# Sums of one column in the free columns of the PV banks, another order of phi and of the residual, and due times found by search

## The chip, the core and the metric

The kernel runs on one core of a Trainium2 chip. Its metric is the device time of one execution in microseconds, the median of three runs. A core has five engines that each work through a queue of their own in order: PE (matrix products, which land in PSUM), ACT (ScalarE, here the exponentials), DVE (VectorE), POOL (GpSimd) and SP, which here only issues DMAs. What one engine needs of another it waits for on a semaphore.

## The reference

Two branches read the same layer-normed input and are added to it. `x` is 2048 x 512, bf16.

```python
xn = layernorm(x)
return x + A(xn) + B(xn)

# A: 32 heads of 16, four segments s of 512 positions, with a memory M, z per head
q, k, v = xn @ wq, xn @ wk, xn @ wv
phi = lambda t: where(t > 0, t + 1.0, exp(t))
p = softmax(q_s @ k_s.T / 4 + mask);  a_dot = p @ v_s
a_mem = phi(q_s) @ M / (phi(q_s) @ z + 1e-6)
o_s = g * a_mem + (1 - g) * a_dot          # g = sigmoid(beta), per head
M = M + phi(k_s).T @ v_s;  z = z + sum(phi(k_s))
A = o @ wo

# B: one position of 2048 goes through a gated MLP
r = xn @ w_r;  idx = argmax(r)
y = (silu(xn[idx] @ w_gate) * (xn[idx] @ w_up)) @ w_down * sigmoid(r[idx])
B = xn, with y added to row idx
```

So the output is `x + xn + A`, with `y` added in one row. `mask` adds -1e9 where the key is later than the query.

## The kernel before, in words

Positions are tiled in 16 blocks of 128; four blocks are a segment. Heads are worked in 16 groups `n` of eight (four groups for each segment), and each group in two units of four heads. A unit is five tiles (`LAYOUT`), so there are 160 tiles in all. A tile is a `score` on PE into `st` (L442, two PSUM buffers), an exponential on ACT into `pt` (L445, six buffers), a mask on POOL (L454), and PV on PE into the unit's bank `acc` (L463, two buffers). PV carries a column of ones, so the bank holds the softmax sums too; DVE reads the unit out with `rr` and `Oseg` (L428, L429). PV fills 272 of the 512 columns of its bank.

PE multiplies all 128 rows of a tile, so a head's queries lie in `QZ`, a tile with zeros outside that head's 16 rows. The projected queries are read out by DVE (`raw_q`, L385), and eight small DMAs from SP scatter them into `QZ` (L379). There are two `QZ` tiles, for even and odd `n`.

`phi` (L368 to L375) takes a projected tile: ACT makes exp(t) into `ex`, POOL clips it into `am`, DVE makes t + 1 and then the maximum of the two. The keys' phi is transposed by DMA (`memT`, L471), and `memM` adds it to the memory; `mem` (L494 to L519) multiplies the memory into a segment's output, and POOL adds that to `Oseg`.

`moe` (L597 to L718) is the branch B. Its products have one column each: the router's 64 (L618), the selected row (L675), gate and up (L690) and down (L709). Each has a bank of the pool `misc`, of which there are two, shared with all projections. `guard` sums squares of the weights likewise (L566); its flag decides on a slow path that these inputs don't take.

`fin` (L536) ends a block of segments 0 to 2: the output is transposed by DMA (`oT`, L541), an identity matmul brings in the row `rb` (L543; POOL makes it from `y` and the layer norm's offset, L524), four matmuls apply `wo` (L545), and DVE adds `x` times `s1` (`ob`, L531). The last segment's four blocks are ended by the code from L869 on; its first two take `x` through three diagonal matmuls (`dg`, L908).

The order of all this on each engine is not written by hand. Every step is an operation of a `Plan`, with the engine, an estimate of its time, what it reads and writes, and a due time `d`. `run` walks a model of the engines: it takes the engine whose next operation can start first, and on that engine, among the operations that can start by then (within 0.03 us, more for some of DVE's), the one with the earliest due time. The result is a fixed queue for each engine; on the chip nothing is reordered. `td(t)` gives the due time of tile `t`.

Of the kernel before, what the change touches and what calls it, by code (L numbers as in the profile page):

```python
# [18 lines left out]
TAIL = {"PE": 0.22, "ACT": 0.18, "DVE": 0.135, "POOL": 0.09, "SP": 1.9}  # L19
# [16 lines left out]
class Plan:  # L36
# [4 lines left out]
    def __init__(self):  # L41
        self.ops = []
        self.writer = {}
        self.readers = {}
        self.floor = {}

# [28 lines left out]
    def run(self, dry=False, log=None):  # L75
        free = {e: 0.0 for e in TAIL}
        port = [0.0]
        nd = {}
# [32 lines left out]
        while left:  # L111
            best = None
            for e, av in avail.items():
# [4 lines left out]
                for o in av:  # L118
# [6 lines left out]
                    if e == "POOL":  # L125
                        t = max(t, port[0])
                    cands.append((t, o))
# [4 lines left out]
                pick = min((o for t, o in cands if t <= lo + (0.8 if o["lock"] and o["d"] < t else 0.03)), key=lambda o: (o["d"], o["id"]))  # L132
# [10 lines left out]
            if o["lock"]:  # L143
                port[0] = end
            fin = end + o["lat"]
# [12 lines left out]
            for u in o["users"]:  # L158
                k = u["id"]
                nd[k] -= 1  # L160
                ready[k] = max(ready[k], end if e == u["eng"] != "SP" else fin)
# [14 lines left out]
def build_kernel(ctx, tc, A_x, A_wq, A_wk, A_wv, A_wo, A_beta, B_x, B_w_r, B_w_gate, B_w_up, B_w_down, out, opts=None):  # L176
# [23 lines left out]
    rot = ctx.enter_context(tc.tile_pool(name="rot", bufs=2))  # L200
# [3 lines left out]
    obp = ctx.enter_context(tc.tile_pool(name="obp", bufs=4))  # L204
# [73 lines left out]
    T0, SL = 11.2, 1.0  # L278
    DTL = 1.35

    def td(t):
        return T0 + SL * t

    class Build:


        def __init__(self, pl, gen):
# [3 lines left out]
            self.prev = dict(s=[], e=[], p=[])  # L291
            self.dq = nc.gpsimd if gen else nc.sync
# [5 lines left out]
        def segt(self, kind, s):  # L298
            if (kind, s) not in self.seg:
                pool, cap, shape = (pk1, 1, [P, 4, D]) if kind == "pk" else (rot, 2, [P, NCB, L])  # L300
                self.seg[(kind, s)] = Buf(pool, cap, shape, bf16, kind)
            return self.seg[(kind, s)]
# [25 lines left out]
        def ln_T(self, b, xb, eng, d):  # L328
            pl = self.pl
            if eng == "DMA":  # L330
                pl.op("SP", 1.26, lambda: nc.sync.dma_start(out=xnT[:, :, b * P:(b + 1) * P], in_=xb[:], transpose=True), r=[xb], w=[("xnT", b)], d=d, lat=DTL)
# [36 lines left out]
        def phi(self, raw, kind, s, j, d):  # L368
            pl = self.pl
            ex, am, tp1 = Buf(phw, 2, [P, L], bf16, "ex"), Buf(phw, 2, [P, L], bf16, "am"), Buf(phw, 2, [P, L], bf16, "tp1")  # L370
            dst = self.segt(kind, s)
            pl.op("ACT", .5, lambda: nc.scalar.activation(out=ex[:], in_=raw[:], func=ACT.Exp), r=[raw], w=[ex], d=d)
# [562 lines left out]
    def slow_path():  # L935
# [3 lines left out]
        def flush():  # L939
            spl.sequence()  # L940
# [120 lines left out]
```

## Time and profile before

| | us |
|---|---|
| median of three runs | 217.96 (217.15 to 219.58) |
| the profiled execution | 219.14 |
| its span, from first to last instruction | 217.4 |
| PE busy | 195.8 |
| ACT busy | 173.1 |
| POOL busy | 149.3 |
| DVE busy | 134.5 |

The rows of the profile are from the one profiled execution. Busy time counts an engine as busy while any of its instructions runs; PE's rows overlap, since matmuls are pipelined. A row of a group of instructions says: line, engine, operation, what is written from what, the shapes, how often; then busy us and mean ns of one; then the idle time of that engine just before, and what ended it. A row of the timeline says start and length in us, then the same names, and in brackets the idle time before it. A row of waits says who waited for whom: us in total, how often, the longest. Names are the program's, without buffer numbers.

### The profile page before, as it was taken

Reading aid. Unit: us, or ns where it says so; the run is one execution under the profiler, and the core shown is the slowest. Engines: PE = TensorE matmul, PEld = TensorE weight load, DVE = VectorE, ACT = ScalarE, POOL = GpSimd, SP = SyncE. Lnnn points to the kernel's source line nnn. Section 1 sums busy time; section 2 is a strip of 40 time slices with the busy share of each in tenths; the row PEclk is TensorE's granted clock in tenths of the full one; section 3 lists DMA queues with packets and bytes.
Section 4 is the critical chain, followed back from the end, with each engine's and each line's share of the span. In section 5 each row is a group of like instructions: output and inputs, shape, how many; then the busy total and the mean of one; then the engine's idle time right before and its main releaser. Section 6 shows DMA issues by size and latency. Waiting matters only on the chain.

```text
span 217.4 us, 6706 instructions
## 1 busy us (share of the span) xinstructions
PE 195.8 (90%) x2598; PEld 128.1 (59%) x2635; DVE 134.5 (62%) x365; ACT 173.1 (80%) x206; POOL 149.3 (69%) x250
## 2 busy tenths in 40 slices
PE   7899798998988999999999999999999799997960
PEld 2656465565646578785676656565666556564620
DVE  5779983465474655997647666446878847653140
ACT  2488988998997689999788796898778679876830
POOL 8018977997983367768669779998876387856500
PEclk9999999999996599999999999999999999999996
DMA  6913994532332413892100432224212102222002
GB/s 179 294 34 113 364 282 80 62 79 53 71 53 48 136 26 85 284 207 73 41 0 19 105 42 64 60 72 65 59 41 57 42 18 59 54 47 54 21 28 87
DMA packets 36985, 19.35 MB, mean 89 GB/s; under 512 B 24976, under 2 KB 36944, under 8 KB 36944
## 3 DMA queue, kind: packets, MB, share of 16 engines
q1 hardware_dynamic: 35840, 18.18, 35.2%
q10 hardware_dynamic: 1104, 0.66, 1.0%
q8 instruction: 22, 0.36, 0.8%
q14 instruction: 19, 0.16, 0.3%
HBM read 9.71 MB, written 2.10 MB: 54 GB/s over the span
## 4 chain that ended last, share of the span: by engine, by line
PE 53%; DMA 13%; DVE 10%; POOL 8%; ACT 6%; issue 4%; SPq 4%; DVEq 0%; ACTq 0%; POOLq 0%
PE st L442 20%; PE acc L463 8%; PE misc L364 6%; DMA QZ<-raw_q 5%; ACT pt L445 5%; PE misc L406 4%; POOL pt L454 4%; DMA xnT<-xn 4%; PE misc L545 3%; DMA pk<-pkT 2%; POOL sq L562 2%; SPq L379 2%; SPq L550 2%; PE misc L690 1%; DMA x_all<-in_A_x_dram 1%
## 5 line engine op out<-in xcount | busy, mean ns | idle before, releaser
L445 ACT ACTIVATE pt<-st 128x1024 bf16<-128x1024 f32 x160 | 154.2, 1028 | 25.8 <-PE st L442 22.5
L454 POOL TENSOR_SCALAR_AFFINE_SELECT pt<-pt 128x512 bf16<-128x512 bf16 (+1 forms) x160 | 88.7, 559 | 52.7 <-ACT pt L445 50.8
L442 PE MATMUL st<-QZ,KT 128*128 128x256 bf16 (+3 forms) x498 | 94.6, 302 | 5.9 <-DMA QZ<-raw_q 4.2
L463 PEld LDWEIGHTS <-pt 128*128 128x128 bf16 x1280 | 49.8, 97 | 20.2 <-POOL pt L454 4.1
L442 PEld LDWEIGHTS <-KT 128*128 128x128 bf16 x512 | 40.2, 98 | 24.0 <-issue 8.0
L463 PE MATMUL acc<-Vaug,pt 128*128 128x17 bf16 x1280 | 53.0, 171 | 1.5 <-DVE rm L512 0.6
L406 PE MATMUL misc<-wv,xnT 128*128 128x512 bf16 x60 | 17.2, 378 | 1.1 <-DMA xnT<-xn 0.9
L428 DVE RECIPROCAL rr<-acc 128x16 f32<-128x16 f32 x32 | 8.0, 250 | 16.4 <-PE acc L463 16.3
L531 DVE SCALAR_TENSOR_TENSOR ob<-x_all,s,misc 128x512 bf16<-128x512 bf16 x12 | 9.0, 748 | 13.9 <-PE misc L545 13.9
L364 PE MATMUL misc<-xnT,wq 128*128 128x512 bf16 x54 | 16.3, 378 | 1.4 <-DVE raw_q L385 1.2
L364 PE MATMUL misc<-xnT,wk 128*128 128x512 bf16 x55 | 16.1, 378 | 0.2
L373 POOL TENSOR_SCALAR am<-ex 128x512 bf16<-128x512 bf16 x24 | 15.1, 631 | 1.5 <-DVE pqT L375 0.5
L385 DVE CAST raw_q<-misc 128x512 bf16<-128x512 f32 x15 | 10.3, 686 | 8.2 <-PE misc L364 3.8
L408 DVE TENSOR_TENSOR Vaug<-misc,omg_bc 128x512 bf16<-128x512 f32 x16 | 10.9, 685 | 5.6 <-PE misc L406 5.3
L429 DVE TENSOR_TENSOR Oseg<-acc,rr 128x256 bf16<-128x256 f32 x32 | 13.5, 423 | 0.9
L524 POOL TENSOR_SCALAR rb<-ybc,onehot,cvec 128x512 bf16<-128x512 bf16 x16 | 12.3, 770 | 1.2 <-PE misc L543 0.9
L519 POOL TENSOR_TENSOR Oseg<-Oseg,om 128x512 bf16<-128x512 bf16 x10 | 11.5, 1155 | 1.9 <-DVE om L514 1.4
L545 PE MATMUL misc<-wo,oT 128*128 128x512 bf16 x42 | 11.8, 378 | 0.2
L308 DVE BATCH_NORM_STATS2 bnst<-x_all 128x6 f32<-128x512 bf16 x16 | 10.7, 666 | 1.5 <-DMA x_all<-in_A_x_dram 1.5
L514 DVE TENSOR_TENSOR om<-misc,rm 128x512 bf16<-128x512 f32 x12 | 8.2, 687 | 5.1 <-PE misc L508 5.1
L396 DVE CAST KT<-misc 128x512 bf16<-128x512 f32 x15 | 10.2, 682 | 1.0 <-PE misc L364 0.6
L324 POOL TENSOR_SCALAR xn<-x_all,rstd,cvec 128x512 bf16<-128x512 bf16 x12 | 9.5, 795 | 0.0
(161 smaller groups left out, 216.9 us busy)
## 6 DMA issues: line engine op xcount, KB each, us to landing
QZ<-raw_q SPq DMA_DIRECT2D x124, 16.0 KB, 1.8
mw<-in_B_w_gate_dram SPq DMA_DIRECT2D x2, 896.0 KB, 5.6
mw<-in_B_w_up_dram SPq DMA_DIRECT2D x2, 896.0 KB, 6.7
mw<-in_B_w_down_dram SPq DMA_DIRECT2D x2, 896.0 KB, 5.7
out_dram<-ob SPq DMA_DIRECT2D x14, 128.0 KB, 2.2
x_all<-in_A_x_dram SPq DMA_DIRECT2D x3, 512.0 KB, 4.7
wv<-in_A_wv_dram SPq DMA_DIRECT2D x1, 512.0 KB, 6.2
wo<-in_A_wo_dram SPq DMA_DIRECT2D x1, 512.0 KB, 4.0
```

The lines of the kernel that those rows point to most:

```text
L364: self.pl.op("PE", .216, lambda cb=cb: nc.tensor.matmul(ps[:], lhsT=w[:, cb, j * P:(j + 1) * P], rhs=xnT[:, cb, s * L:(s + 1) * L], start= ...
L373: pl.op("POOL", .58, lambda: nc.gpsimd.tensor_scalar(out=am[:], in0=ex[:], scalar1=1.0, scalar2=0.0, op0=ALU.min, op1=ALU.max), r=[ex], w= ...
L406: self.pl.op("PE", .216, lambda cb=cb: nc.tensor.matmul(ps[:], lhsT=xnT[:, cb, b * P:(b + 1) * P], rhs=wv[:, cb, :], start=(cb == 0), stop ...
L408: o = self.pl.op("DVE", .62, lambda: nc.vector.tensor_tensor(out=Vaug[:, b, :, 0:DH], in0=ps[:].rearrange("p (h e) -> p h e", e=DH), in1=o ...
L429: pl.op("DVE", .345, lambda: nc.vector.tensor_tensor(out=Oseg[s][:, :, j, 4 * w:4 * w + 4, :], in0=av()[:, :, :, 0:DH], in1=rr[:, :, :, No ...
L442: nc.tensor.matmul(st[:, i, off:off + n], lhsT=lh, rhs=QZ[q][:, h, q0:q0 + n], start=True, stop=True)
L445: self.prev["e"] = [pl.op("ACT", .907, lambda: nc.scalar.activation(out=pt[:], in_=st[:], func=ACT.Exp, scale=SCALE), r=[st], w=[pt], afte ...
L454: nc.gpsimd.affine_select(out=mv, in_=mv, pattern=pat, compare_op=ALU.is_ge, fill=0.0, base=0, channel_multiplier=-1)
L463: nc.tensor.matmul(acc[:, q0 // P + c, i, e, :], lhsT=pt[:, i, off + c * P:off + (c + 1) * P], rhs=Vaug[:, 4 * s + kb, h, :], start=first, ...
L519: pl.op("POOL", 1.12, lambda: nc.gpsimd.tensor_tensor(out=Oseg[s][:, :, j], in0=Oseg[s][:, :, j], in1=om[:], op=ALU.add), r=[om], w=[("O", ...
L524: self.pl.op("POOL", .75, lambda: nc.gpsimd.tensor_scalar(out=t[:], in0=small_t["ybc"][:], scalar1=small_t["onehot32"][:, b:b + 1], scalar ...
L545: pl.op("PE", .216, lambda cb=cb: nc.tensor.matmul(fin[:], lhsT=oT[:, cb, :], rhs=wo[:, cb, :], start=False, stop=(cb == NCB - 1)), r=[oT, ...
```

## The change

Six things change.

- The one-column sums of `moe` and `guard` get no bank of their own. They write into columns 272 and up of the bank of a unit (`V["moe"]` and `V["guard"]` name the units), after that unit's first PV; the unit's read-out waits for them.
- `phi` becomes max(t + 1, exp(min(t, 0))): DVE makes the minimum ahead of ACT's exponential, and POOL's clipping is gone.
- POOL makes the whole residual `x * s1 + cvec` in f32 (`xr`); `fin` has four matmuls, DVE adds `y` times the row's flag to the product in PSUM, and then the residual. In the tail `y` is added to `xr`, and two blocks take `xr` through two matmuls, as a bf16 part and the rest.
- DVE adds the memory's part to `Oseg` in POOL's place.
- Some heads of a group (`dvp`, 27 in all over n = 1 to 15) get their `QZ` by a multiplication on DVE in place of a DMA.
- The due times come from a table `V`, and some of the model's estimates change. Four of the MLP's weight tiles may be loaded at once (three before).

```diff
-TAIL = {"PE": 0.22, "ACT": 0.18, "DVE": 0.135, "POOL": 0.09, "SP": 1.9}
+TAIL = {"PE": 0.22, "ACT": 0.18, "DVE": 0.16, "POOL": 0.09, "SP": 1.9}
+SAME = {"PE": 0.0, "ACT": 0.0, "DVE": 0.11, "POOL": 0.0, "SP": 0.0}
...
-    rot = ctx.enter_context(tc.tile_pool(name="rot", bufs=2))
+    rot = ctx.enter_context(tc.tile_pool(name="rot", bufs=3))
+    xrp = ctx.enter_context(tc.tile_pool(name="xrp", bufs=2))
+    xrt = ctx.enter_context(tc.tile_pool(name="xrt", bufs=4))
...
-    mwp = ctx.enter_context(tc.tile_pool(name="mwp", bufs=3))
+    mwp = ctx.enter_context(tc.tile_pool(name="mwp", bufs=4))
...
+    V = dict(
+        dvp=(0, 2, 2, 2, 2, 2, 2, 2, 3, 3, 1, 1, 2, 1, 1, 1), dvl=1.826, slack=0.696, near=0.0, thin=0.204, sl=1.061, pq=8.672, pk=3.155, ev=-0.218,
...
-    T0, SL = 11.2, 1.0
-    DTL = 1.35
+    T0, SL = 11.2, V["sl"]
+    DTL = 1.4
...
+    XC = 4 * 4 * (DH + 1)
...
-            pl.op("ACT", .5, lambda: nc.scalar.activation(out=ex[:], in_=raw[:], func=ACT.Exp), r=[raw], w=[ex], d=d)
-            pl.op("POOL", .58, lambda: nc.gpsimd.tensor_scalar(out=am[:], in0=ex[:], scalar1=1.0, scalar2=0.0, op0=ALU.min, op1=ALU.max), r=[ex], w=[am], d=d + 1)
+            pl.op("DVE", .22, lambda: nc.vector.tensor_scalar(out=mn[:], in0=raw[:], scalar1=0.0, scalar2=None, op0=ALU.min), r=[raw], w=[mn], d=d + V["phmn"], lock=True)
...
+            pl.op("ACT", .5, lambda: nc.scalar.activation(out=ex[:], in_=mn[:], func=ACT.Exp), r=[mn], w=[ex], d=d)
...
+            nd = V["dvp"][n] if self.gen == 0 else 0
+            for h in range(nd):
+                self.pl.op("DVE", .22, lambda h=h: nc.vector.tensor_scalar(out=QZ[q][:, h, :], in0=raw[:], scalar1=bdsel[:, h:h + 1], scalar2=None, op0=ALU.mult),
+                           r=[raw], w=[("QZ", q, h)], d=td(10 * n + (5 if h >= 4 else 0)) - V["dvl"], lock=True)
...
-            acc = Buf(psa, 2, [P, 4, 2, 2, DH + 1], f32, "acc")
+            acc = Buf(psa, 2, [P, L], f32, "acc")
+            hook, keys = self.hooks.pop(base // 5, None) if self.gen == 0 else None, []
...
+                if k == 0 and hook:
+                    keys = hook[0](acc, self.prev["p"], td(t) + 2.5)
...
-            pl.op("POOL", 1.12, lambda: nc.gpsimd.tensor_tensor(out=Oseg[s][:, :, j], in0=Oseg[s][:, :, j], in1=om[:], op=ALU.add), r=[om], w=[("O", s, j, 0), ("O", s, j, 1)], d=d + 5)
+            pl.op("DVE", .37, lambda: nc.vector.tensor_tensor(out=Oseg[s][:, :, j], in0=Oseg[s][:, :, j], in1=om[:], op=ALU.add), r=[om], w=[("O", s, j, 0), ("O", s, j, 1)], d=d + V["madd"], lock=True)
...
-            self.pl.op("POOL", .75, lambda: nc.gpsimd.tensor_scalar(out=t[:], in0=small_t["ybc"][:], scalar1=small_t["onehot32"][:, b:b + 1], scalar2=cvec[:, b:b + 1], op0=ALU.mult, op1=ALU.add),
+            self.pl.op("POOL", .8, lambda: nc.gpsimd.tensor_scalar(out=t[:], in0=x_all[:, b, :], scalar1=s1[:, b:b + 1], scalar2=cvec[:, b:b + 1], op0=ALU.mult, op1=ALU.add), r=[("s1", b), ("cvec", b)], w=[t], d=d)
...
+            pl.op("DVE", .66, lambda: nc.vector.scalar_tensor_tensor(out=sub(fin), in0=small_t["ybc"][:], scalar=small_t["onehot32"][:, b:b + 1], in1=sub(fin), op0=ALU.mult, op1=ALU.add),
+            o = pl.op("DVE", .66, lambda: nc.vector.tensor_tensor(out=t[:], in0=sub(fin), in1=xr[:], op=ALU.add), r=[fin, ("fy", b), xr], w=[t], d=d)
...
-            pl.op("PE", .216, lambda: nc.tensor.matmul(fin[:], lhsT=ident[:], rhs=rb[:], start=True, stop=False), r=[rb, oT], w=[fin], d=d + 1)
...
+            def sums(acc, first, d, step, groups, r, name):
+                keys = []
+                for g, mk in enumerate(groups):
+                    def mm(mk=mk):
+                        for c, lh, rh in mk():
+                            nc.tensor.matmul(acc[:, XC + c:XC + c + 1], lhsT=lh, rhs=rh, start=False, stop=True, skip_group_check=True)
...
+        if qb < 2:
+            terms = [("xh", lambda o, h=h, st=st: nc.tensor.matmul(o, lhsT=ident[:], rhs=h[:], start=st, stop=False), [h]) for h, st in ((hl[qb][0], True), (hl[qb][1], False))]
```

What stands in the queues then, at three places. First SP's queue at the start: `x_all` is the input, `mw` the MLP's weights, `QZ_136` and `QZ_137` the queries of even and odd groups (`QZ_145` and `QZ_146` after the change). Before:

```order
L748 DMA wk<-in_A_wk_dram 128x4x384
L766 DMA x_all<-in_A_x_dram 128x4x512
L379 DMA QZ_136<-raw_q 16x512 x4
L766 DMA x_all<-in_A_x_dram 128x4x512
L379 DMA QZ_137<-raw_q 16x512 x4
L766 DMA x_all<-in_A_x_dram 128x4x512
L379 DMA QZ_137<-raw_q 16x512
L610 DMA mw<-in_B_w_gate_dram 128x4x896
L379 DMA QZ_137<-raw_q 16x512 x3
```

And after the change:

```order
L808 DMA wk<-in_A_wk_dram 128x4x384
L659 DMA mw<-in_B_w_gate_dram 128x4x896
L826 DMA x_all<-in_A_x_dram 128x4x512
L659 DMA mw<-in_B_w_gate_dram 128x4x896
L410 DMA QZ_145<-raw_q 16x512 x4
L826 DMA x_all<-in_A_x_dram 128x4x512
L659 DMA mw<-in_B_w_up_dram 128x4x896 x2
L826 DMA x_all<-in_A_x_dram 128x4x512
L824 DMA wr_col<-in_B_w_r_dram 128x4x1
L410 DMA QZ_146<-raw_q 16x512 x6
```

Two weight tiles moved ahead of the scatters of the first group, and two more ahead of those of the second, of which there are six in place of eight.

Second, SP's queue at the end: `QZ_137` (then `QZ_146`) are the queries of the last group, `oT_144` (then `oT_153`) the transposed output of the last segment, `oT` that of the one before, `out_dram` the output. Before:

```order
L379 DMA QZ_137<-raw_q 16x512
L550 DMA_TRANSPOSE oT_144<-Oseg_143 128x2x128
L379 DMA QZ_137<-raw_q 16x512
L550 DMA_TRANSPOSE oT_144<-Oseg_143 128x2x128
L379 DMA QZ_137<-raw_q 16x512 x2
L550 DMA_TRANSPOSE oT_144<-Oseg_143 128x2x128 x2
L379 DMA QZ_137<-raw_q 16x512 x4
L533 DMA out_dram<-ob 128x512 x2
```

And after the change:

```order
L410 DMA QZ_146<-raw_q 16x512 x4
L583 DMA_TRANSPOSE oT<-Oseg_151 128x4x128
L410 DMA QZ_146<-raw_q 16x512
L575 DMA out_dram<-ob 128x512
L410 DMA QZ_146<-raw_q 16x512 x2
L583 DMA_TRANSPOSE oT<-Oseg_151 128x4x128
L591 DMA_TRANSPOSE oT_153<-Oseg_152 128x2x128
L575 DMA out_dram<-ob 128x512
L591 DMA_TRANSPOSE oT_153<-Oseg_152 128x2x128 x3
```

The four transposes of the last segment moved behind the last scatters.

Third, DVE's queue around the projected queries (`raw_q`) of the last group. Before:

```order
L514 TENSOR_TENSOR om<-misc,rm 128x512 x2
L385 CAST raw_q<-misc 128x512
L374 TENSOR_SCALAR tp_4224<-raw_q 128x512
L531 SCALAR_TENSOR_TENSOR ob<-x_all,s_154,misc 128x512
L396 CAST KT<-misc 128x512
L428 RECIPROCAL rr<-acc 128x16
```

And after the change (`tp_4004` belongs to the group before):

```order
L551 TENSOR_SCALAR rm<-misc 128x32
L468 TENSOR_TENSOR Oseg_152<-acc,rr 128x4x64
L553 RECIPROCAL rm<-rm 128x32
L403 TENSOR_SCALAR mn<-raw_q 128x512
L421 TENSOR_SCALAR QZ_146<-raw_q,bdsel 128x512
L555 TENSOR_TENSOR om<-misc,rm 128x512
L406 TENSOR_TENSOR pqT<-tp_4004,ex 128x512
L572 SCALAR_TENSOR_TENSOR misc<-ybc,onehot_179,misc 128x512
L952 CAST xn<-xr 128x512
L574 TENSOR_TENSOR ob<-misc,xr 128x512
L431 CAST KT<-misc 128x512
L467 RECIPROCAL rr<-acc 128x16
```

The minimum (L403), a query multiplication (L421), the step on PSUM ahead of `ob` (L572) and a cast for the tail (L952) now stand among the read-outs of PSUM.

More of the change, by code (lines that the diff above doesn't have):

```diff
@@ L144, in run @@
                 port[0] = end
+            if o["cols"] is not None and o["cols"] < 10:
+                thin[0] = end + self.thin
             fin = end + o["lat"]
@@ L812, in build_kernel @@
     pl.op("DVE", .3, gates2, r=["eb"], w=["ecol"], d=40)
+    B.moe(V["moe"])
+    B.guard(V["guard"])
     for n in range(16):
```

448 lines of the change are left out of this document (229 added, 219 removed).

## The prediction

> **What bounds the kernel now.** I read the page's head, then the busy time of stages, then the waits. A row of stages holds: stretch, its length, then busy us (and instructions) of PE, PEld, DVE, ACT and POOL, the granted PE clock, the share of the DMA engines and GB/s.
>
> ```profile
> span 217.4 us, 6706 instructions
> PE 195.8 (90%) x2598; PEld 128.1 (59%) x2635; DVE 134.5 (62%) x365; ACT 173.1 (80%) x206; POOL 149.3 (69%) x250
> 12.00:208.00 196.00, 183.61 (x2514) 121.67 (x2549) 124.58 (x340) 167.68 (x196) 144.15 (x236) 0.97 0.36 82
> 100.00:160.00 60.00, 58.75 (x768) 38.06 (x778) 37.27 (x94) 51.37 (x59) 49.84 (x78) 1.00 0.24 50
> 66.00:78.00 12.00, 10.90 (x155) 7.85 (x153) 7.71 (x31) 8.80 (x12) 4.35 (x8) 0.57 0.33 84
> 80.00:100.00 20.00, 19.73 (x399) 15.24 (x400) 15.14 (x45) 19.50 (x23) 15.22 (x26) 1.00 0.73 174
> ACT pt L445 <- PE st L442: 22.5, 32, 1.9
> PE st L442 <- DMA QZ<-raw_q: 4.2, 6, 1.2
> ```
>
> The loop of 160 score tiles runs from about 12 to 208 us. In it ACT, which takes the exponentials, is busy 167.68 of 196 us, so 28.3 us of it stand idle; the waits row says that 22.5 of ACT's idle time ended with a score matmul. So ACT waits for PE, and what counts is why the scores come late. Three reasons show. In 100 to 160 us PE is full (58.75 of 60) and ACT is not (51.37). In 66 to 78 us PE ran at 0.57 of its clock. And PE itself waited 4.2 us, in six places, for the scattered queries (QZ). In 80 to 100 us both engines are nearly full, so there is nothing to win there without less work. The span can fall only by what fills those 28.3 us, or by the 12 us before and 9 us after the loop.
>
> The profiled execution took 219.14 us, 1.74 more than its span; the median of the three runs, 217.96, is 1.18 less than the profiled time. I forecast the span and add 0.56 for the median.
>
> **The change part by part.**
>
> *PE loses work.* The residual row `rb` no longer enters through an identity matmul, and the first two blocks of the tail no longer take `x` through three diagonal matmuls.
>
> ```profile
> L543 PE MATMUL misc<-rb,ident 128*128 128x512 bf16 x12 | 4.5, 377 | 0.1
> L543 PE MATMUL misc<-rb,ident x7: 376/377/379, 117.4 to 154.5; 128*128 128x512 bf16 x7
> L908 PE MATMUL misc<-x_all,dg 128*128 128x512 bf16 x6 | 1.8, 378 | 0.0
> L894 PE MATMUL misc<-rb,ident x2: 376/378/379, 198.5 to 203.7; 128*128 128x512 bf16 x2
> 117.78 0.86 PE misc L545 x4
> ```
>
> Removed: 12, 4 in the tail (two into `misc` as in the last but one row, two more into `st`) and 6, together 22 matmuls of 512 columns; added: 4 (the high and low halves of the residual for two blocks); net 18. One reads as 377 ns, but they overlap: four in a row on the chain took 0.86, so 0.215 each, 3.9 us in all. Seven of them stood in 100 to 160 us, where PE is full: 1.5 us in full. The other 11 count half: 1.2. I take -2.7, with ends -3.9 and 0.
>
> *The one-column sums.* The 328 matmuls of one column keep their price; they move from banks of their own to the unused columns of a PV bank, in groups of 4 to 8 between scores and PV (on PE the router's sums now stand in 13 groups around seven score tiles). Before, the router's 64 stood in one block:
>
> ```profile
> 63.45 0.39 PE L442 MATMUL st<-QZ,KT 128*128 128x512 bf16 x1
> 64.72 0.38 PE L442 MATMUL st<-QZ,KT 128*128 128x512 bf16 x1 [0.87 <-DMA QZ<-raw_q]
> ...
> 65.15 1.76 PE L618 MATMUL misc<-wr_col,xnT 128*128 128x1 bf16 x64
> 66.78 1.01 PE L442 MATMUL st<-QZ,KT 128*128 128x128 bf16 x4
> ```
>
> From 63.45 to 66.78 us PE had a few wide matmuls, a wait and that block, and then the clock was down for some 11 us. Had 66 to 78 us run at full clock, PE's 10.90 us would have been 10.90 x 0.57, 4.7 less; ACT's idle time there is 12 - 8.80 = 3.2. I take -3.2 for a dip that does not come back, with ends -4.7 and 0. [...] What is late next: PV of the unit that holds the sums cannot be read out before its last sum, and only two such banks exist; I count that at nothing, since the units after it still have one.
>
> *The scatters.* Of the DMAs that scatter the queries 27 become DVE multiplications (124 issues before, 97 now), at the first heads of each block. And at the end of SP's queue the four transposes of the last segment now stand behind all scatters of the last block.
>
> ```profile
> 191.04 1.25 SPq L550
> ...
> 194.88 1.45 SPq L550
> 197.65 3.06 DMA QZ<-raw_q
> 201.22 3.86 ACT L445 ACTIVATE pt<-st 128x1024 bf16<-128x1024 f32 x4 [1.85 <-PE st L442]
> ```
>
> The chain ran through these transposes, 1.25 us or more each, to the last scatter, and ACT stood 1.85. I take -1.5 (ends -1.85 and 0; one older transpose and one output still stand among the last scatters). Of PE's 4.2 us of waiting for QZ, 0.87 belong to the dip and 1.2 to this place; of the other 2.1 I take -1.0, with ends -2.1 and 0.
>
> *DVE gains work.*
>
> ```profile
> L374 DVE TENSOR_SCALAR tp<-raw_q 128x512 bf16<-128x512 bf16 x12 | 4.3, 358 | 0.0
> L374 DVE TENSOR_SCALAR tp<-KT 128x512 bf16<-128x512 bf16 x12 | 3.8, 313 | 0.0
> L830 DVE TENSOR_SCALAR QZ<-raw_q,bdsel 128x512 bf16<-128x512 bf16 x2 | 0.6, 351 | 0.1
> L375 DVE TENSOR_TENSOR pkT<-tp,am 128x512 bf16<-128x512 bf16 x12 | 5.9, 492 | 0.9 <-POOL am L373 0.5
> L531 DVE SCALAR_TENSOR_TENSOR ob<-x_all,s,misc 128x512 bf16<-128x512 bf16 x12 | 9.0, 748 | 13.9 <-PE misc L545 13.9
> L903 DVE CAST dg<-dres 128x128 bf16<-128x128 f32 x6 | 2.2, 366 | 0.2
> L905 DVE TENSOR_TENSOR dres<-dres,dg 128x128 f32<-128x128 f32 x4 | 2.1, 523 | 0.1
> L901 DVE TENSOR_SCALAR dres<-ident,s 128x128 f32<-128x128 f32 x2 | 1.0, 480 | 0.0
> PE misc L364 <- DVE raw_q L385: 1.2, 1, 1.2
> ACT ex L372 <- DVE KT L396: 1.5, 1, 1.5
> ```
>
> Added: 24 minima like `tp`, 24 x 0.336 = 8.1; 27 query multiplications x 0.351 = 9.5; 10 memory additions like `pkT` x 0.492 = 4.9; 12 additions of y in PSUM x 0.748 = 9.0; for the tail four more, two casts and two subtractions, 6 x 0.748 + 2 x 0.366 = 5.2. Removed: the diagonals, 5.3. Net 31.4. In the loop DVE goes from 124.6 to 156 us; in a loop of 188 us that is 83% where it was 64%. Nearly all of it can lie beside other work, since DVE has idle time for it; but work queued behind it comes later. PE and ACT waited 2.7 us for DVE's read-outs in the two rows above. If such waits grow as DVE's idle share falls, from 36% to 17%, they double: +2.7. Ends 0 and +8, a quarter of the added work.
>
> POOL loses 24 minima and 10 additions:
>
> ```profile
> L373 POOL TENSOR_SCALAR am<-ex 128x512 bf16<-128x512 bf16 x24 | 15.1, 631 | 1.5 <-DVE pqT L375 0.5 <-ACT pt L445 0.4 <-DVE rm L510 0.4
> L519 POOL TENSOR_TENSOR Oseg<-Oseg,om 128x512 bf16<-128x512 bf16 x10 | 11.5, 1155 | 1.9 <-DVE om L514 1.4 <-DVE hs L581 0.5
> POOL pt L454 <- ACT pt L445: 50.8, 79, 8.7
> 163.62 1.16 DVE L582 TENSOR_TENSOR hs<-hs 8x4 f32<-8x4 f32 x1
> ```
>
> That is 26.6 us off an engine which waited 50.8 us for ACT: nothing. The last row shows what DVE pays beside POOL: an operation on 8x4 numbers took 1.16 us, from the same instant as one of the ten additions on POOL. [...]
>
> *Weights earlier.* Four weight transfers of 896 KB now stand ahead of the scatters of the second block, two of them even ahead of those of the first.
>
> ```profile
> 8.00:10.00 2.00, 2.00 (x27) 1.50 (x26) 1.30 (x4) 1.14 (x2) 0.00 (x0) 1.00 1.07 352
> mw<-in_B_w_gate_dram SPq DMA_DIRECT2D x2, 896.0 KB, 5.6
> QZ<-raw_q SPq DMA_DIRECT2D x124, 16.0 KB, 1.8
> QZ<-raw_q SPq DMA_DIRECT2D x3, 16.0 KB, 6.4
> 34.92 1.94 ACT L445 ACTIVATE pt<-st 128x1024 bf16<-128x1024 f32 x2 [1.02 <-PE st L442]
> ```
>
> Before, three scatters issued at 27.6 us behind such weights landed after 6.4 us instead of 1.8, and ACT lost 1.02 at 34.92. The two weights ahead of the first scatters are 1.83 MB, 5.2 us at the 352 GB/s of the first row. That loss moves forward rather than grows: 0, ends -1 and +3.
>
> *The tail.* The second block's sum is now ended last on PE and its output is a third on SP: 2 x 0.215 more, and part of one issue: +0.6, ends 0 and +1.
>
> *The due times.* What else the new order does cannot be read from a trace of the old one. Of ACT's 28.3 us idle, some 21 are left without the dip, the last scatters and the waits for QZ. I take about a sixth of it, -3.3; the ends, -9 and +9, are the unknown of this forecast.
>
> Sum: -2.7 - 3.2 - 1.5 - 1.0 + 2.7 + 0 + 0.6 - 3.3 = -8.4. Span 209.0, time 209.6.
>
> **The rivals.**
>
> 1. *The loop closes up.* ACT's idle time falls by half, 14.1 us: span 203.3, time 203.9. For it: PE, ACT and POOL all have room outside 80 to 120 us. Against: PE and ACT are coupled through two score banks. 0.18.
> 2. *The change does not do what it says.* PE's freed time is only half on the path, the dip comes back somewhere (new gaps behind DVE), and the new order gives nothing: -1.35 - 1.5 - 1.0 + 2.7 + 0.6 = -0.5, time 217.4. 0.14.
> 3. *DVE becomes the bound, slower.* No 20 us stage has DVE above 15.14 (76%). If that is what its chains of read-outs, waiting for PSUM and for POOL, let through, 156 us of work need 206 us instead of the loop's 196: span 227, time 228; half way, 222. It decides where the added work comes in lumps on the read-outs of PSUM, in the blocks with two phi chains and where the output sums start, and from a DVE share of about 80% on. For it: 31 us is much. Against: 15.14 is what was asked of DVE, not what it can do. 0.13.
>
> **How the numbers follow.** My forecast has 0.55, with its own range 205 to 214.5. Within 1% means 215.8 to 220.1, about what a measurement can tell. Faster: 0.55 + 0.18 = 0.73; same 0.14; slower 0.13. The range goes down into the first rival and up over the second, 202.5 to 218, and leaves the third out.
>
> **What would show it.** Right: PE's clock at 1.00 throughout 60 to 80 us; ACT's wait for scores under 16 us; waits for QZ under 2; PE's busy time about 4 us less; DVE near 166. Wrong: ACT or PE waiting for DVE by 6 us or more (third rival); a new low-clock stretch; a wait for QZ of over 2 us before 30 us (the weights).

## The result, and the profile after

The changed kernel took 208.08 us (median of four runs, 207.58 to 209.13). The kernel before took 217.96 (217.15 to 219.58); the ratio is 0.954, with a 95% interval of 0.946 to 0.962. So it is faster, and the forecast of 209.6 us was 1.5 us too high. A further run of the kernel before took 224.88 us; as a run more than 1.5% above the fastest of its kernel, it is left out, and so are such runs in all ratios below. The profiled execution took 209.13 us with a span of 207.4, which is 10.0 less than the span before.

First the head of the page of after:

```profile
span 207.4 us, 6692 instructions
PE 189.3 (91%) x2617; PEld 125.3 (60%) x2617; DVE 155.4 (75%) x426; ACT 171.7 (83%) x206; POOL 126.5 (61%) x216
```

Then its stages, in the columns of the prediction: the loop to 196 us, and the three stages that were shown of before.

```profile
12.00:196.00 184.00, 174.84 (x2523) 117.80 (x2522) 146.04 (x401) 166.48 (x196) 121.31 (x202) 1.00 0.35 84
66.00:78.00 12.00, 11.17 (x218) 8.57 (x216) 8.21 (x27) 12.00 (x15) 7.60 (x14) 1.00 0.25 52
80.00:100.00 20.00, 19.63 (x367) 15.07 (x365) 17.92 (x61) 19.49 (x26) 10.28 (x18) 1.00 0.23 46
100.00:160.00 60.00, 59.55 (x843) 39.74 (x842) 50.33 (x128) 54.26 (x64) 38.83 (x63) 1.00 0.32 70
```

In the loop ACT now stands idle 184 - 166.48 = 17.5 us, where it was 28.3. From 66 to 78 us ACT has no gap at all, and PE's clock is at 1.00. From 100 to 160 us PE is as full as before, but ACT does 54.26 us of work there in place of 51.37, since more of what PE does is scores: 168 products into `st` start there, where it was 152.

The waits of after, as who waited for whom:

```profile
ACT lnv L344 <- DVE MV L339: 7.0, 2, 3.5
ACT pt L486 <- PE acc L504: 5.3, 6, 2.2
ACT pt L486 <- PE st L483: 4.3, 8, 1.1
ACT ob L981 <- DMA out_dram<-ob: 2.8, 1, 2.8
ACT ex L405 <- DVE mn L403: 2.7, 3, 2.1
PE misc L394 <- DVE KT L431: 2.2, 1, 2.2
```

ACT's wait for a score fell from 22.5 us to 4.3. No wait of PE for `QZ` of 0.2 us or more is left. New is a wait of ACT for PV (`acc`, 5.3): an exponential cannot overwrite a `pt` that PV has not yet read.

Where the 10.0 us came from is read off ACT's last exponentials. The first fence is ACT's timeline of before, the second that of after, with the tail:

```profile
205.94 1.02 ACT L445 ACTIVATE pt<-st 128x1024 bf16<-128x1024 f32 x1 [0.85 <-PE st L442]
```

```profile
189.69 5.60 ACT L486 ACTIVATE pt<-st 128x1024 bf16<-128x1024 f32 x6
197.76 0.37 ACT L938 CAST oT<-acc 128x256 bf16<-128x256 f32 x1 [2.47 <-PE acc L933]
198.62 0.59 ACT L981 CAST ob<-misc 128x512 bf16<-128x512 f32 x1 [0.49 <-PE misc L975]
202.04 0.59 ACT L981 CAST ob<-misc 128x512 bf16<-128x512 f32 x1 [2.83 <-DMA out_dram<-ob]
```

The last exponential ended at 206.96 us before and at 195.29 after: the loop gained 11.7 us. From there to the end of the span it was 10.4 us before and 12.1 after: the tail lost 1.7. In the tail of after ACT stands 2.83 us before its second cast, waiting for an output DMA.

The way there is not even. The stages from 20 to 80 us, first of before, then of after:

```profile
20.00:40.00 20.00, 17.67 (x234) 11.53 (x236) 14.81 (x40) 17.65 (x24) 16.30 (x30) 1.00 0.89 209
40.00:60.00 20.00, 18.49 (x236) 11.71 (x238) 10.31 (x26) 19.13 (x25) 17.05 (x28) 1.00 0.32 65
60.00:80.00 20.00, 17.57 (x272) 12.52 (x273) 13.06 (x45) 15.32 (x19) 10.28 (x18) 0.74 0.30 70
```

```profile
20.00:40.00 20.00, 15.91 (x195) 9.72 (x194) 16.71 (x52) 14.35 (x21) 12.97 (x24) 1.00 0.57 142
40.00:60.00 20.00, 18.45 (x227) 11.51 (x224) 12.01 (x28) 17.69 (x20) 18.11 (x30) 1.00 0.28 58
60.00:80.00 20.00, 18.58 (x317) 13.36 (x316) 11.17 (x37) 19.86 (x23) 13.87 (x23) 1.00 0.37 80
```

By 60 us the kernel before has started 42 of its 160 exponentials, the changed kernel only 35; by 80 us it is 54 and 55. So the changed kernel first falls behind by seven, and makes this up in the stage in which the kernel before has its dip.

The longest wait in the part that went worse stands in ACT's timeline of after:

```profile
23.22 2.96 ACT L486 ACTIVATE pt<-st 128x1024 bf16<-128x1024 f32 x3 [0.49 <-PE acc L504]
29.68 0.30 ACT L344 ACTIVATE lnv<-MV,eps_col 128x4 f32<-128x4 f32 x1 [3.51 <-DVE MV L339]
```

and the DMA issues of after (count, KB each, median us from issue to landing):

```profile
x_all<-in_A_x_dram SPq DMA_DIRECT2D x3, 512.0 KB, 8.4
mw<-in_B_w_up_dram SPq DMA_DIRECT2D x2, 896.0 KB, 8.7
```

ACT waits 3.51 us for the statistics of a late third of the input, which is queued behind two of the weights.

### The profile page after: what moved, and what is told of

Its sections match the earlier page's. It is cut to its first block, busy times and chain, and to the rows that moved or that the text cites. A ratio compares the mean times of both kernels' runs of the same rounds, so it can differ in the third digit from the quotient of the medians.

```text
span 207.4 us, 6692 instructions
## 1 busy us (share of the span) xinstructions
PE 189.3 (91%) x2617; PEld 125.3 (60%) x2617; DVE 155.4 (75%) x426; ACT 171.7 (83%) x206; POOL 126.5 (61%) x216
## 4 chain that ended last, share of the span: by engine, by line
PE 56%; ACT 15%; DMA 15%; DVE 5%; issue 4%; POOL 2%; SPq 1%; ACTq 0%; DVEq 0%
PE st L483 23%; ACT pt L486 14%; PE acc L504 9%; PE misc L394 9%; DMA mw<-in_B_w_gate_dram 5%; PE misc L441 4%; DMA x_all<-in_A_x_dram 4%; PE misc L586 3%; DMA wq<-in_A_wq_dram 3%; PE acc L680 2%; DMA xnT<-xn 2%; POOL pt L495 1%; DMA out_dram<-ob 1%; PE misc L522 1%; PE misc L549 1%
## 5 line engine op out<-in xcount | busy, mean ns | idle before, releaser
L504 PEld LDWEIGHTS <-pt 128*128 128x128 bf16 x1280 | 45.3, 96 | 13.9 <-POOL pt L495 2.0
L504 PE MATMUL acc<-Vaug,pt 128*128 128x17 bf16 x1280 | 48.7, 171 | 0.1
L394 PE MATMUL misc<-xnT,wk 128*128 128x512 bf16 x60 | 18.9, 378 | 2.2 <-DVE KT L431 2.2
L394 PE MATMUL misc<-xnT,wq 128*128 128x512 bf16 x60 | 18.0, 378 | 2.1 <-DMA xnT<-xn 1.2
L405 ACT ACTIVATE ex<-mn 128x512 bf16<-128x512 bf16 x24 | 15.4, 643 | 3.2 <-DVE mn L403 2.7
L467 DVE RECIPROCAL rr<-acc 128x16 f32<-128x16 f32 x32 | 8.0, 250 | 12.1 <-PE acc L504 8.5
L431 DVE CAST KT<-misc 128x512 bf16<-128x512 f32 x15 | 10.2, 683 | 5.2 <-PE misc L394 4.1
L586 PE MATMUL misc<-wo,oT 128*128 128x512 bf16 x48 | 13.4, 379 | 0.0
L443 DVE TENSOR_TENSOR Vaug<-misc,omg_bc 128x512 bf16<-128x512 f32 x16 | 10.8, 681 | 3.4 <-PE misc L441 3.2
L565 POOL TENSOR_SCALAR xr<-x_all,s,cvec 128x512 f32<-128x512 bf16 x16 | 12.8, 799 | 0.2 <-DVE ob L574 0.2
L572 DVE SCALAR_TENSOR_TENSOR misc<-ybc,onehot,misc 128x512 f32<-128x512 bf16 x12 | 9.0, 747 | 5.2 <-PE misc L586 5.1
L680 PEld LDWEIGHTS <-mw 128*128 128x128 bf16 x168 | 8.4, 96 | 3.8
L421 DVE TENSOR_SCALAR QZ<-raw_q,bdsel 128x512 bf16<-128x512 bf16 x27 | 10.3, 410 | 0.0
```

The source lines that it names most:

```text
L394: self.pl.op("PE", .216, lambda cb=cb: nc.tensor.matmul(ps[:], lhsT=w[:, cb, j * P:(j + 1) * P], rhs=xnT[:, cb, s * L:(s + 1) * L], start= ...
L443: o = self.pl.op("DVE", .62, lambda: nc.vector.tensor_tensor(out=Vaug[:, b, :, 0:DH], in0=ps[:].rearrange("p (h e) -> p h e", e=DH), in1=o ...
L504: nc.tensor.matmul(accv(acc)[:, q0 // P + c, i, e, :], lhsT=pt[:, i, off + c * P:off + (c + 1) * P], rhs=Vaug[:, 4 * s + kb, h, :], start= ...
L565: self.pl.op("POOL", .8, lambda: nc.gpsimd.tensor_scalar(out=t[:], in0=x_all[:, b, :], scalar1=s1[:, b:b + 1], scalar2=cvec[:, b:b + 1], o ...
L586: pl.op("PE", .216, lambda cb=cb: nc.tensor.matmul(fin[:], lhsT=oT[:, cb, :], rhs=wo[:, cb, :], start=(cb == 0), stop=(cb == NCB - 1)), r= ...
L680: nc.tensor.matmul(acc[:, XC + c:XC + c + 1], lhsT=lh, rhs=rh, start=False, stop=True, skip_group_check=True)
```

## The experiments

Times are medians; ranges are of the runs of that kernel. The kernels were run in three sets, each with runs of the kernel before beside it. Only the set of the tail and the early weights holds the changed kernel again (208.56 us). The kernel before took 219.16 us there, 219.15 in the set of the router's sums and of DVE's doubled work, and 217.12 in the set of the 18 products, the planned run, the old due times and the queries, so differences across sets are uncertain by about 2 us.

### What PE's work is worth

**18 products put back.**

```diff
+                if cb == 0:
+                    nc.tensor.matmul(fin[:], lhsT=zero_t[:, 0:P], rhs=zero_t[:], start=True, stop=False)
...
```

(and six more in the tail's sums)

> The changed kernel, with 18 products of 512 columns put back on PE (zeros: one ahead of each of the 12 products with wo, six in the tail's sums); all else keeps its place. Theory (my step for PE's work: of 3.9 us some 2.7 are on the path): 211.0 us. Rivals: all on the path, 212.2; none, because ACT or DVE sets the pace in that stretch, 208.5.

Measured: 212.21 us (212.05 to 212.64), 4.1 above the changed kernel's 208.08 and 3.7 above its second measurement, 208.56. The 18 products are 18 x 0.215 = 3.9 us of PE's time. Not all of the difference need be theirs: in the profiled execution, 212.05 us, the clock is 0.91 on average from 20 to 40 us. In the profiled execution of the changed kernel above it is 1.00 there; in that of its second measurement, 209.05 us, it is 0.91 likewise, and beside that one 3.0 us are left. So 3.0 to 4.1 us: most of PE's work was on the path, perhaps all of it, and my step of 2.7, which counted 11 of them half, was somewhat low.

### What the clock is worth, and what lowers it

**The router's sums in one block again, in after.**

```diff
-                    def mm(mk=mk):
-                        for c, lh, rh in mk():
+                    def mm(mk=mk, g=g):
+                        if name == "r" and g:
+                            return
+                        for c, lh, rh in [x for m in (groups if name == "r" else [mk]) for x in m()]:
```

> The changed kernel, with the router's 64 one-column products issued in one block, where the first group of four stood; all else keeps its place in the queues. Theory (a block of thin products lets the clock fall, as I priced the dip of before): the granted clock falls to about 0.6 for some 10 us behind the block, near 50 to 70 us, and the time grows by 3 us or more, to 211. Rival (the dip of before needed its waits beside the block, or was none of its doing): the clock stays at 1.00, and the time is within 1 us of 208.3.

**The router's block filled, in before.**

```diff
...
-                    for cb in range(NCB):
-                        nc.tensor.matmul(r_ps[:, b:b + 1], lhsT=xnT[:, cb, b * P:(b + 1) * P], rhs=wr_col[:, cb:cb + 1], start=(cb == 0), stop=(cb == NCB - 1))
+                    if b % 2 == 0:
+                        nc.tensor.matmul(r_ps[:], lhsT=zero_t[:, 0:P], rhs=xnT[:, b // 4, 0:L], start=True, stop=True)
...
```

> The kernel before, with the router's 64 one-column products replaced by eight products of 512 columns (the router's sums are left out, so the chosen row is another): the block lasts 1.7 us as before, but PE is filled in it. Theory (the thin block makes the dip): the clock stays near 1.00 in 60 to 80 us, and the time falls by about 3.2 us, to 215. Rival (the wait for the scatters and the few products around it make the dip, or the clock falls whatever PE does): the dip stays and the time is that of before, 218.

The block in after: 209.49 us (208.68 to 210.57), and the clock in the profiled execution (208.75 us) stayed at 1.00 throughout the loop. That is 0.9 to 1.4 us more, not 3. Of the three runs without a profile one had a lower mean clock, 0.976, than any of the changed kernel's, so a dip in that one can't be excluded. The filled block in before: 218.16 us (213.89 to 220.46), a ratio to before of 1.005 (0.988 to 1.021): no difference shows. In its profiled execution the dip did not go, it came later. Stages of this kernel:

```profile
74.00:92.00 18.00, 17.63 (x290) 12.40 (x288) 8.66 (x29) 13.46 (x16) 10.56 (x17) 0.62 0.57 141
76.00:88.00 12.00, 12.00 (x195) 8.49 (x192) 4.67 (x16) 9.11 (x9) 6.92 (x12) 0.50 0.40 111
```

and PE's timeline where it begins:

```profile
73.43 0.64 PE L675 MATMUL misc<-onehot,x_all 128*128 128x1 bf16 x20
73.93 0.34 PE L463 MATMUL acc<-Vaug,pt 128*128 128x17 bf16 x8
74.13 0.24 PE L675 MATMUL misc<-onehot,x_all 128*128 128x1 bf16 x4
74.74 0.38 PE L678 MATMUL misc<-selr,ones 128*128 128x2 f32 x2 [0.37 <-DVE om L514]
74.98 0.44 PE L675 MATMUL misc<-onehot,x_all 128*128 128x1 bf16 x12
```

The clock falls at about 75.9 us, behind the next thin products of the branch B, those of the selected row. So neither theory stands as I put it: with the thin block in after the clock stayed at 1.00, and with the router's block filled in before it fell to 0.50 behind the next thin stretch. Each is one profiled execution. What lowers the clock is left open by both runs.

What a low clock costs can be read from the runs of before. There are 35 of them beside these experiments, all counted here, from 213.32 us at a mean granted clock of 0.996 to 225.53 us at 0.937. A straight line through them gives 1.50 us for each 0.01 of the mean clock and 214.4 us at full clock; the correlation is 0.90. Their mean clock is 0.969; that of the ten runs of the changed kernel is 0.991. (The mean takes in the end of the execution, where PE is mostly idle and the clock is low as well: in the profiled execution of the changed kernel, from 196 us on, PE is busy for 3.67 of 11.40 us at a clock of 0.90. That execution, at 0.994, has no dip in its loop.) The difference, 0.022, is worth 3.3 us by this line. The line shows that time and clock go together, not that the clock alone costs this: a wait of PE in which the clock falls, as that of 6.40 us in the kernel with the weights later (below), is lost time itself. Within the ten runs of the changed kernel, whose mean clocks lie between 0.984 and 0.995 only, no such line shows (correlation +0.30).

### What DVE's work and the due times are worth

**Phi's minimum and t + 1 made twice**, with the queues left as they are, and once more with the doubled price made known to the planner:

```diff
-            pl.op("DVE", .22, lambda: nc.vector.tensor_scalar(out=mn[:], in0=raw[:], scalar1=0.0, scalar2=None, op0=ALU.min), r=[raw], w=[mn], d=d + V["phmn"], lock=True)
...
+            pl.op("DVE", .22, lambda: [nc.vector.tensor_scalar(out=mn[:], in0=raw[:], scalar1=0.0, scalar2=None, op0=ALU.min) for _ in range(2)], r=[raw], w=[mn], d=d + V["phmn"], lock=True)
...
```

(`tp1` likewise; in the second kernel the model's 0.22 for each becomes 0.44)

> The changed kernel, with phi's minimum and t + 1 each made twice by DVE (48 operations, some 14 to 16 us of work more, nothing else moved). Theory (what DVE gains costs PE and ACT little; 2.7 us for 31 us was my price): 1.0 to 1.5 us more, time 209.6. Rival (DVE's chains are already the bound, each us of its work counts for a third or more): 5 us or more, time 213 or above.

> The minimum and t + 1 made twice, as in the run that took 222.8 us, but now the planner counts both at the doubled price, and lays the queues accordingly (the table of due times stays). Theory (the price of DVE's work is that of a fixed order that does not know of it): well under half of the 14 us remain, 214 us or less. Rival (DVE cannot carry 175 us of work beside what it must be in time for): 220 us or more.

Measured: 222.83 us (221.92 to 223.30) with the old queues, and 227.71 (226.19 to 228.96) with new ones. The page's head of the first:

```profile
span 220.9 us, 6735 instructions
PE 194.3 (88%) x2617; PEld 127.1 (58%) x2617; DVE 175.0 (79%) x474; ACT 173.7 (79%) x206; POOL 126.7 (57%) x216
```

and its waits, to be read beside those of after:

```profile
ACT pt L486 <- PE st L483: 9.5, 15, 2.5
ACT pt L486 <- PE acc L504: 7.4, 7, 2.2
ACT ex L405 <- DVE mn L403: 6.1, 5, 3.2
```

DVE has 175.0 - 155.4 = 19.6 us more to do, and the time grows by 14.3 us (against 208.56): 0.73 us for each us. Part of that goes with a lower clock, 0.966 on average where the changed kernel's is 0.991: by the line above 3.9 of the 14.3 us. Whether DVE's work caused the lower clock is not shown; without that part the price is 10.4 / 19.6 = 0.53. My forecast had 2.7 for 31.4, less than 0.09. What comes later is not only what waits for DVE itself (`ex`, from 2.7 to 6.1): scores and PV come late too (from 9.6 to 16.9), most likely since a projection that DVE has not read out holds one of the two `misc` banks, and PE's queue stands behind it. Letting the planner know made it worse, most likely since the table of due times had been searched for another set of costs, and a new walk with it gave a poorer order. So this run does not show that a better order for 175 us of DVE's work does not exist; it shows that the order is not found by correcting a price.

**The old due times, with all changed operations.**

```diff
+    V.update(dict(slack=0.8, near=0.03, thin=0.12, sl=1.0, pq=8.0, pk=4.0, ev=1.0, evv=1.0, sc0=3.0, sc4=3.0, phq=1.0, phk=3.0, phmn=-1.0, phtp=1.0, phmx=2.0,
+                  score=0.9, mask=1.1, pv=2.2, rr=3.3, pv0=-1.0, pv1=2.0, pv2=2.0, pv3=2.0, pvs=1.2, mt=2.0, mt3=2.0, mm=7.0, mrun=0.5, mbf=2.0, zbf=2.0,
...
```

> All of the changed kernel's operations, with the due times of the kernel before wherever both have the operation (slope 1.0, slack 0.8, and some 45 entries of the table). Theory by my forecast (the order as such gives 3.3 us): 211.6 us. Rival, after the run in which DVE's phi was made twice (the new times are what makes room for DVE's added work, and without them each us of it costs 0.7): DVE's added 20 us cost some 14, and the time goes to 218 or above.

Measured: 220.41 us (219.42 to 221.94); the ratio to before is 1.016, with an interval of 1.004 to 1.028, so it is no faster than the kernel before, and by the interval slightly slower. Its waits:

```profile
ACT pt L490 <- PE st L487: 16.7, 26, 1.7
ACT ex L409 <- DVE mn L407: 7.2, 3, 4.2
PE misc L445 <- DVE QZ L425: 2.6, 1, 2.6
```

ACT's wait for scores is back at 16.7 us, beside waits for DVE that before did not have. With DVE busy for 153.0 us (after: 155.4) it is the same work in another order. So the due times are worth 11.9 to 12.3 us to the changed operations, of which some 2 go with a lower clock (0.977 on average) by the line above; and the other edits gain nothing with the old times. Entries of the table that only the changed kernel has, the early weights among them, kept their new values here.

**No queries by DVE.**

```diff
-        dvp=(0, 2, 2, 2, 2, 2, 2, 2, 3, 3, 1, 1, 2, 1, 1, 1), dvl=1.826, slack=0.696, near=0.0, thin=0.204, sl=1.061, pq=8.672, pk=3.155, ev=-0.218,
+        dvp=(0,) * 16, dvl=1.826, slack=0.696, near=0.0, thin=0.204, sl=1.061, pq=8.672, pk=3.155, ev=-0.218,
```

> The changed kernel with all 124 scatters by DMA again, so 27 multiplications fewer on DVE (11 us of its busy time) and 27 more DMAs from SP; the planner lays the queues anew. Theory by my forecast (1.0 us for the waits for the queries, against 0.8 for DVE's work): 208.5 us. Rival one (DVE's work costs 0.7 per us): 7 us less, 201. Rival two (SP's queue is too full, and PE waits for the queries as before, 4 us): 212.

Measured: 213.83 us (212.59 to 214.99), 5.3 to 5.7 above the changed kernel, though DVE has less to do. PE's own wait for `QZ` returned with 2.1 us, ACT's for scores is 10.8 (after 4.3). This lies nearest to the second rival. But the queues were laid anew here, as in the planned run above, so the price of 27 scatters and that of another order cannot be told apart.

### The tail and the early weights

Four kernels. First the changed kernel again, then the tail's output tiles from a pool of four buffers:

> The changed kernel itself, once more, beside its two repairs: 208.1 us, as before. It is the base from which the runs beside it are counted.

```diff
-        tt = Buf(obp, 3, [P, D], bf16, "ob")
+        tt = Buf(sqp, 4, [P, D], bf16, "sq")
```

> The changed kernel, with the four output tiles of the tail in a pool of four buffers that is idle by then, not in the output pool of three; the queues are the same. In the trace of after, ACT's second cast stands 2.83 us for an output DMA to give its buffer back, and its own output DMA is the last instruction. Theory (this wait is on the path): the cast starts at the end of the block's last product, near 199.7 in place of 202.04, but SP then still has two other outputs to issue: 1.3 to 2.3 us less, time 206.3. Rival (the end is set by the outputs' issue and landing, whichever is last): less than 0.5 us, time 207.9.

Then the weights due later, alone (`lmw=22.0` in place of 6.129) and with the tail's buffer:

> The changed kernel, with the four weight transfers of 896 KB due at 22 us and later, as before the change; all queues but SP's are the same, and there the input's last two thirds now go ahead of the weights. In the trace of after, the input's last transfer took 8.4 us to land, DVE waited 1.93 for it and ACT 3.51 behind that, at 26.2 us. Theory (the early loss is this, and the rest of the queues shifts as one): 2 to 3 us less, time 205.6. Rival (the weights still stand ahead of the second block's scatters, and what is gained early is lost there or in the full stretch from 80 to 160 us): less than 1 us, time 207.5.

> Both repairs, of the tail's buffer and of the weights. Theory: they lie at the two ends of the program and add up, 3.5 to 5 us less than the changed kernel, time 203.9. Rival: one of them is hidden, time 206 to 207.

And, after these, the up weights alone moved far behind, with the tail's buffer:

```diff
-                pl.op("SP", .61, go, w=[t], d=dd, e=min(dd, 16.0), lat=6.0)
+                pl.op("SP", .61, go, w=[t], d=dd, e=min(dd, 16.0) if kind == "g" else dd, lat=6.0)
...
-                load_mw(kind, hf, V["lmw"] + 4 * i)
+                load_mw(kind, hf, V["lmw"] + 4 * i if kind == "g" else (40., 52.)[hf])
```

> The changed kernel with the tail's output tiles in four buffers, the two gate weights where the change puts them, the input's last third ahead of the up weights, and the two up weights far behind: behind the second block's scatters (due at 40 and 52 us). Theory (ACT's early loss is the input's last third behind the up weights, and the loss of the run with all weights later was the second block's scatters behind four weights): both losses go, 2 to 3 us less than with the tail's buffer alone, 203.5 us. Rival (the early stretch is set by PE and by DVE's read-outs anyway): within 1 us of 206.2.

| kernel | median, us | range | ratio to before |
|---|---|---|---|
| the changed kernel again | 208.56 | 207.18 to 209.74 | 0.953 (0.947 to 0.959) |
| tail's buffer | 206.19 | 205.59 to 207.44 | 0.944 (0.939 to 0.948) |
| weights later | 212.51 | 211.70 to 213.37 | 0.973 (0.968 to 0.977) |
| both | 210.39 | 209.88 to 212.30 | 0.964 (0.958 to 0.969) |
| up weights far behind, tail's buffer | 204.63 | 203.62 to 206.90 | 0.936 (0.930 to 0.943) |

The tail's buffer gives 2.4 us (2.1 beside the later weights). ACT's tail of that kernel:

```profile
199.80 0.36 ACTq L983 DMA_DIRECT2D out_dram<-sq  x1
200.26 0.59 ACT L981 CAST sq<-misc 128x512 bf16<-128x512 f32 x1 [0.49 <-PE misc L975]
```

The cast now follows its product. So the wait of 2.83 us was on the path, and it came from one line of the change that I passed over: the output pool shrank from four buffers to three.

Weights due later lost 4.0 us where I expected 2 to 3 of gain, and lost it elsewhere. ACT's wait at 26 us did shrink (to 1.29 us), but PE's timeline of this kernel shows:

```profile
26.28 0.35 PE L504 MATMUL acc<-Vaug,pt 128*128 128x17 bf16 x8
33.04 1.03 PE L441 MATMUL misc<-wv,xnT 128*128 128x512 bf16 x2 [6.40 <-DMA xnT<-xn]
```

The layer norm's transposes of the second segment now stand behind all four weights, and PE waits 6.40 us for them; the clock, which fell in that gap, reads 0.50 from 29 to 38.5 us and is low until 38.9. The mean clock of this kernel's runs is 0.972, and by the line above the low clock goes with some 2.9 of the 4.0 us. My rival had named the second block's scatters; it was the transposes behind these. So to have the weights early, as the change has them, is right by 4 us against the late place tried here.

With the up weights alone far behind, ACT is busy 17.38 us from 20 to 40 us. The first stage is of the changed kernel run again, where it was 13.91 (14.35 in the profile further up), the other two of this kernel:

```profile
20.00:40.00 20.00, 16.46 (x175) 9.37 (x173) 15.36 (x50) 13.91 (x20) 12.51 (x24) 0.91 0.56 137
```

```profile
20.00:40.00 20.00, 18.96 (x225) 11.43 (x223) 17.68 (x55) 17.38 (x25) 15.29 (x25) 1.00 0.31 60
40.00:60.00 20.00, 16.62 (x190) 10.11 (x189) 10.27 (x24) 14.50 (x16) 14.93 (x23) 0.91 0.46 105
```

In the next stage, 40 to 60 us, ACT has 14.50 us only. POOL's and PE's timelines of this kernel tell why:

```profile
48.41 0.77 POOL L354 TENSOR_SCALAR xn<-x_all,rstd,cvec 128x512 bf16<-128x512 bf16 x1 [2.40 <-DMA xnT<-xn]
```

```profile
49.83 0.36 PE L504 MATMUL acc<-Vaug,pt 128*128 128x17 bf16 x8 [1.89 <-POOL pt L495]
```

The early loss is gone. But a transpose behind the first up weight came late, POOL waited 2.40 us for it from 46 us on, and the mask queued behind on POOL held up PV by 1.89. In that execution the gain of the first stage was lost in the second: by 60 us 35 exponentials have started, as in the changed kernel. It is also the longest of this kernel's six runs, 206.90 us, and its mean clock, 0.988, the lowest; the others have 0.994 to 0.999. The median, 204.63, is 1.6 below that of the tail's buffer alone, but the two were run in different sets and their intervals overlap (0.930 to 0.943 and 0.939 to 0.948). It is the fastest of all kernels here, 3.5 us below the changed kernel.

## Why the prediction was right, step by step

The sum came out at -8.4, and -10.0 is what the profiled span lost. The total is better than its terms, and that is luck: two large ones were wrong and nearly cancel.

**PE's work: -2.7 taken, 3.0 to 4.1 measured.** The mechanism was right and the size somewhat low. Outside 100 to 160 us I counted the freed work half, because PE has gaps there; but PE works in a fixed queue, and a product in front of a score can delay that score though there is a gap later. That this is the reason is argued, not shown.

**The dip: -3.2 taken, 3.3 by the clock.** The size agrees as far as the line goes. The cause that I gave, the router's block, was not shown: as one block in after it cost about a us and, in the profiled execution, no clock, and filled up in before it left a dip. Nor can this term be told from others in the profiles: from 60 to 80 us, where before has its dip, the changed kernel made up the seven exponentials by which it was behind. By the mean clocks, 0.937 to 0.996 in the 35 runs of before and 0.984 to 0.995 in the ten of the changed kernel, low clock comes more or less often, and the changed kernel has less of it. Why less is argued, not shown: PE waits less for others.

**The scatters: -1.5 and -1.0 taken.** The waits for `QZ` are gone in the trace, as forecast, and ACT's last six exponentials run without a gap. The run without DVE's queries lost 5.3 us or more, but with a new order, so these 2.5 us are consistent with the runs and not measured by them.

**DVE's work: +2.7 taken; this step failed.** Two errors. The busy time grew by 20.9 us, not 31.4, because I added up mean durations, and DVE's operations overlap. The timeline of after:

```profile
30.21 0.27 DVE L403 TENSOR_SCALAR mn<-KT 128x512 bf16<-128x512 bf16 x1
30.40 0.28 DVE L404 TENSOR_SCALAR tp<-KT 128x512 bf16<-128x512 bf16 x1
30.60 0.61 DVE L421 TENSOR_SCALAR QZ<-raw_q,bdsel 128x512 bf16<-128x512 bf16 x2
```

They start 0.19 and 0.20 us apart, though each reads 0.27 or 0.28. For PE I had corrected for that, for DVE not. The larger error is the price. Work that is put into this fixed order cost 0.73 us per us when it was measured (0.53 if all that goes with the lower clock is taken off), not 0.09. That is the mechanism of my third rival, and the time of the run, 222.8 at a DVE share of 79%, is that rival's half way (222, "from a DVE share of about 80% on"). The change stays at 75%, and its order was laid for this work. My sign for that rival, PE or ACT waiting for DVE by 6 us or more, was crossed all the same: 7.0 + 2.7 + 2.2 = 11.9 us in the rows above, of which 3.5 belong to the late input. It was too weak a sign: the waits of that kind summed to 7.2 before, by the two rows of the prediction and this one:

```profile
ACT lnv L314 <- DVE MV L309: 4.5, 2, 3.4
```

**The due times: -3.3 taken; this step failed in size.** The old times cost 12 us (some 10 without what goes with the lower clock), beyond my end of 9. Read together with the step before: the changed operations without the new times lie 2 to 3 us above the kernel before, and with them 10 below. I had treated the two as independent terms, one known and one unknown. They are one: what added work costs depends on whether the order was laid for it.

**Weights: 0 taken, -1 to +3.** The early loss was there (3.51 us at 26 us), not at the scatters that I named but at the input behind the up weights; moving these weights gained 1.6 at most so far. The whole early part is further behind than this one wait: 35 exponentials by 60 us, where it was 42, and no profiled kernel here with the changed operations has more than 39. My 0 passed over that; how much of it is the weights and how much the new order, these runs don't tell. Against the late place tried, the change's place gains 4.0, which my range did not hold.

**The tail: +0.6 taken; 1.7 measured from the last exponential on.** I priced the two more products and the third output on SP, and missed the buffer. With four buffers 2.4 us are gone.

**POOL: 0, and the signs.** Nothing in the waits of after speaks against the 0. The clock at 1.00 from 60 to 80 us, ACT's wait for scores under 16 us and `QZ` under 2 came as written. PE's busy time fell by 6.5 us in place of 4, the rest most likely the dip, which had stretched it: a score of 512 columns took 603 ns on average from 67 to 76 us, where before has its dip, and 378 from 100 to 160. DVE near 166 us was wrong, by the overlap. And the sign of a new low-clock stretch was crossed in the second profile of the changed kernel, with 3.4 us between 32 and 40 us, though not in the first.

## What to carry to other kernels

In queues of fixed order, added work and the order that places it are one term: price them together, or bound the sum by a run with only one of them. An engine at 75% busy, as DVE is here, can still be one whose next us costs half to three quarters of a us (0.53 to 0.73): what counts, as far as these runs show, is when its results are due. Read a diff for pool sizes as closely as for operations: one buffer fewer cost 2.4 us here.

## What the runs showed of the hardware

In the dips read here, within the loop, the clock fell for whole multiples of one length, 3.4 us. Stages around four dips, of before, of the changed kernel run again, and of the kernels with the weights later and with the up weights far behind:

```profile
64.00:80.00 16.00, 13.80 (x223) 10.23 (x224) 9.26 (x37) 11.32 (x15) 6.62 (x13) 0.68 0.31 77
```

```profile
32.00:40.00 8.00, 6.79 (x60) 3.73 (x60) 4.94 (x14) 6.05 (x9) 4.83 (x9) 0.79 0.30 62
```

```profile
26.00:42.00 16.00, 9.24 (x84) 4.92 (x83) 8.23 (x28) 7.22 (x11) 4.66 (x8) 0.68 0.60 124
```

```profile
48.00:56.00 8.00, 6.17 (x73) 3.89 (x74) 3.04 (x7) 3.17 (x4) 6.21 (x10) 0.79 0.30 65
```

Inside these dips, and in that of the filled block, slices of half a us read a clock of 0.50. So the time spent low is 2 x (1 - clock) x length: 2 x 0.32 x 16 = 10.2 us, 3.4, 10.2 and 3.4; the dip of the filled block is 2 x 0.38 x 18 = 13.7. These are one, three and four times 3.4 us. Why it is this length, and why the changed kernel has a dip in one profiled execution (0.91 from 20 to 40 us) and none in the other (1.00), is not shown. In the filled block's kernel PE was busy, as the profile counts it, for 12.00 of 12.00 us from 76 to 88 us, and the clock stayed at 0.50. And the last of the four dips follows a gap of PE of 1.89 us (its row is shown above).
